# Layer one's pair 2 moved from lone periods into the teams, in a kernel of channel attention and two GLU layers

## The chip, the core and the metric

One NeuronCore of a Trainium2 chip runs the whole program. The metric is the device time of one execution in microseconds; the time of before is the median of three runs, 1169.1 us (1168.38 to 1170.15). Engines are named as in the profile: PE is TensorE's matmul, DVE VectorE, ACT ScalarE, POOL GpSimd, SP the engine that issues most DMAs.

## The reference

There are 6016 tokens with 256 channels. Three things follow each other:

```python
qn = q / (norm(q, axis=1) + 1e-6); kn = k / (norm(k, axis=1) + 1e-6)
a = softmax(kn.T @ qn / tau); x = v @ a              # 256 x 256 attention over channels
x = rmsnorm(x) * rms_g                               # layer one: d_ff = 1536
x = (silu(x @ w_gate) * (x @ w_val)) @ w_out
x = (sigmoid(x @ w2_gate) * (x @ w2_val)) @ w2_out   # layer two: d_ff = 1536
```

All is float32. PE multiplies in a split form: each operand is a high part (float32r) and a low rest, and a product is three matmuls (high x high, high x low, low x high; `mm3`).

## The kernel before, in words

**Blocks, pairs, tiles of weights.** The 47 tiles of 128 tokens form twelve blocks of 512 (block 5 has 384). Two blocks are a pair; pair 2 has 448 columns in each half (`hw`), the others 512. The hidden width is cut into NF = 12 tiles f of 128.

**Stages.** First the attention (until about 104 us), then layer one's pairs 0 and 1 as *plain items*: 48 items (block, f), each with 12 matmuls for gate and value and, two items later (SKEW), 6 for the output. The items of blocks 0 and 1 alternate, then come blocks 2 and 3. Under the plain items the weights of both layers are converted (`conversion`: from 64-bit numbers to float32 by ACT and DVE, sums of weight blocks by POOL, then high by ACT and low by DVE). The steps of a conversion stand in five groups (`ORDER`); a deque `steps` holds the groups of all conversions, and `quota` (lines 1171 to 1181) says how many groups an item pumps, from what is left until item `end`, and from when each tile of layer one is due. Hooks hang further work on single items.

**Double blocks.** Every other pair of both layers is computed with Winograd's form of Strassen's product: seven products (A11, S1, S2, A12, S3, S4, A22) in place of eight. A period is one (layer, pair, f). Seven products of three matmuls are 21 matmuls. The intermediate values live in PSUM banks Z, B, A, D; between two products that use one bank, ACT copies it out (`cpA`, `cpG`, `cpD` and so on).

**Lone and team periods.** Layer one's pair 2 (`PLAIN = 2`) runs first, in twelve lone periods (`period`, line 772). The hidden values are split into parts, and the output layer is computed directly, 4 x 3 = 12 matmuls per f. These periods also prepare layer one's six output weight pairs and the first three of layer two: `out_load`, `out_high`, `out_low`, `out_sums`, with stores to `od`; and they store layer one's weights (`store_w`). Then come nine pairs in *teams* (`team_period`, line 843): six f are one team, and its output product too has Winograd's form, 7 kinds x 3 products x 3 = 63 matmuls per six f. A team's output products run during the six periods after it. So the first six team periods have none of their own; they follow the list `NONE`, and the odd ones take their Z and B from the spare `at` banks. The weights of a team period are read from DRAM two periods ahead (`gw_load`, into three tiles), those of the output product by `ow_load`; partial sums of hidden values go by accumulating DMAs from POOL (`more`, line 604).

**What sets the order.** Everything is emitted in a hand-written order; each engine works its queue in that order, and SP issues DMAs in that order too, so an issue that waits holds all behind it. `slots` hang the next pair's loads, sums and splits and the output weights on points of a period (`early`, `ACT`, `DVE`, `end`).

## Time and profile before

| what | us |
|---|---|
| median of three runs | 1169.1 |
| the profiled execution | 1170.04 |
| its span, first to last instruction | 1168.3 |
| PE busy | 1148.7 |
| DVE busy | 968.3 |
| ACT busy | 890.2 |
| POOL busy | 334.3 |

A busy PE is not a PE at its peak: matmuls are pipelined and counted with their overlap, so the distance between their starts tells more. An idle time stands in brackets with the instruction that ended it. TensorE's granted clock was 0.996 over the span.

### The profile page before, as it was taken

How to read it: one execution, taken by the hardware profiler on the slowest of the kernel's cores; microseconds unless marked ns; L12 is line 12 of the kernel's file. 1: busy time of each engine (PE TensorE's matmuls, PEld its weight loads, DVE VectorE, ACT ScalarE, POOL GpSimd, SP SyncE). 2: the span in 40 equal slices, each digit the busy share in tenths (PEclk: the TensorE clock that was granted, in tenths of full speed). 3: DMA queues.
4: the chain of work that ended last, by engine and by line, in shares of the span. 5: the costliest groups of instructions: out<-in, count | busy, mean ns of one | idle time of the engine just before them, and what ended most of it. 6: DMA issues, size and time to landing. Idle time of an engine off the chain costs nothing.

```text
span 1168.3 us, 16678 instructions
## 1 busy us (share of the span) xinstructions
PE 1148.7 (98%) x5236; PEld 957.0 (82%) x5236; DVE 968.3 (83%) x1496; ACT 890.2 (76%) x1664; POOL 334.3 (29%) x398
## 2 busy tenths in 40 slices
PE   8899999999999999999999999999999999999998
PEld 7788788888898778888888788888888888888896
DVE  6798999886667688888888887888888888888877
ACT  6666788775577687887787887787787787787685
POOL 0043677454223322321321321311311321321121
PEclk9899999999999999999999999999999999999999
DMA  9663445867489989999999998998998998998995
GB/s 329 241 220 143 145 148 190 282 228 238 145 280 322 355 258 266 303 264 266 303 262 272 300 258 251 287 265 245 288 265 240 293 260 247 293 261 245 284 273 147
DMA packets 142856, 296.84 MB, mean 254 GB/s; under 512 B 13872, under 2 KB 53168, under 8 KB 142768
## 3 DMA queue, kind: packets, MB, share of 16 engines
q1 hardware_dynamic: 122032, 258.65, 65.6%
q0 software_dynamic: 20592, 37.00, 18.1%
q8 instruction: 41, 0.67, 0.2%
q14 instruction: 47, 0.39, 0.1%
q10 hardware_dynamic: 144, 0.13, 0.0%
HBM read 201.98 MB, written 56.75 MB: 221 GB/s over the span
## 4 chain that ended last, share of the span: by engine, by line
PE 84%; DVE 8%; DMA 4%; issue 2%; ACT 2%; POOL 1%; SPq 0%; DVEq 0%; POOLq 0%; ACTq 0%
PE g L107 12%; PE g L109 12%; PE g L108 12%; PE v L107 6%; PE v L108 6%; PE v L109 6%; PE y L108 5%; PE y L109 5%; PE y L107 5%; PE at L108 4%; PE at L107 4%; PE at L109 4%; DMA in<-in_q_dram 1%; PE y L973 1%; DVE xn L329 1%
## 5 line engine op out<-in xcount | busy, mean ns | idle before, releaser
L605 POOL DMA_DIRECT2D hs<-hs x143 | 124.7, 918 | 571.5 <-DVE hl L688 413.6
L688 DVE TENSOR_TENSOR hl<-hs,hh 128x512 fp32r<-128x512 f32 (+1 forms) x319 | 221.1, 704 | 25.1 <-ACT hh L657 24.2
L657 ACT CAST hh<-hs 128x512 fp32r<-128x512 f32 (+1 forms) x319 | 192.6, 615 | 25.7 <-PE at L109 6.5
L874 ACT COPY v<-g 128x512 f32<-128x512 f32 (+1 forms) x210 | 119.0, 567 | 63.1 <-PE g L109 59.8
L879 DVE TENSOR_TENSOR hs<-g,e 128x512 f32<-128x512 f32 (+1 forms) x105 | 71.5, 681 | 66.5 <-ACT v L874 65.6
L107 PE MATMUL g<-xh,gw 128*128 128x512 f32 x240 | 94.1, 392 | 0.7 <-DVE hs L879 0.6
L108 PE MATMUL g<-xl,gw 128*128 128x512 f32 x240 | 93.5, 389 | 0.0
L109 PE MATMUL g<-xh,gw 128*128 128x512 f32 x240 | 93.4, 389 | 0.0
L908 ACT ACTIVATE g<-g 128x512 f32<-128x512 f32 (+1 forms) x108 | 67.5, 625 | 30.4 <-DVE g L912 29.4
L107 PE MATMUL y<-hh,ow 128*128 128x512 f32 (+1 forms) x211 | 81.7, 387 | 0.2 <-issue 0.2
L108 PE MATMUL y<-hl,ow 128*128 128x512 f32 (+1 forms) x211 | 81.7, 387 | 0.0
L109 PE MATMUL y<-hh,ow 128*128 128x512 f32 (+1 forms) x211 | 81.6, 387 | 0.0
L874 ACT COPY g<-g 128x512 f32<-128x512 f32 (+1 forms) x105 | 61.3, 583 | 26.2 <-PE g L109 25.8
L912 DVE TENSOR_TENSOR g<-g,g 128x512 f32<-128x512 f32 (+1 forms) x105 | 70.3, 669 | 5.7 <-PE g L109 5.7
L883 ACT ACTIVATE sg<-v 128x512 f32<-128x512 f32 (+1 forms) x108 | 64.2, 594 | 7.5
L107 PE MATMUL g<-qh,gw 128*128 128x512 f32 (+1 forms) x171 | 66.5, 389 | 0.7 <-DVE hs L879 0.6
L109 PE MATMUL g<-qh,gw 128*128 128x512 f32 (+1 forms) x171 | 65.8, 385 | 0.0
L108 PE MATMUL g<-ql,gw 128*128 128x512 f32 (+1 forms) x171 | 65.8, 385 | 0.0
L108 PE MATMUL at<-hl,ow 128*128 128x512 f32 (+1 forms) x160 | 62.4, 390 | 0.6 <-DVE hl L688 0.6
L107 PE MATMUL at<-hh,ow 128*128 128x512 f32 (+1 forms) x160 | 62.2, 389 | 0.3 <-ACT hh L657 0.2
L109 PE MATMUL at<-hh,ow 128*128 128x512 f32 (+1 forms) x160 | 61.9, 387 | 0.0
L874 ACT COPY e<-g 128x512 f32<-128x512 f32 (+1 forms) x105 | 61.3, 584 | 0.4
(256 smaller groups left out, 3312.4 us busy)
## 6 DMA issues: line engine op xcount, KB each, us to landing
gw<-gd SPq DMA_DIRECT2D x216, 448.0 KB, 5.6
ow<-od SPq DMA_DIRECT2D x126, 384.0 KB, 5.4
hs<-hs POOLq DMA_DIRECT2D x128, 256.0 KB, 7.7
wraw<-in_w_dram SPq DMA_DIRECT2D x24, 768.0 KB, 5.3
od<-o SPq DMA_DIRECT2D x48, 256.0 KB, 4.6
vraw<-in_v_t_dram SPq DMA_DIRECT2D x11, 512.0 KB, 4.9
gd<-w2h SPq DMA_DIRECT2D x12, 448.0 KB, 2.6
gd<-w2l SPq DMA_DIRECT2D x12, 448.0 KB, 3.6
```

Source lines behind the costliest of these rows:

```text
L107: nc.tensor.matmul(ps, sh, mh, start=start, stop=False, skip_group_check=more)
L108: nc.tensor.matmul(ps, sh, ml, start=False, stop=False, skip_group_check=more)
L109: nc.tensor.matmul(ps, sl, mh, start=False, stop=stop, skip_group_check=more)
L329: nc.vector.tensor_scalar_mul(xn[b][:, i], ps[i // 2][:, i % 2], rs[:, i : i + 1])
L605: nc.gpsimd.dma_start(out=to, in_=t, accum_op=ALU.add)
L657: nc.scalar.copy(h, src)
L688: nc.vector.tensor_sub(lo, src, f32(h))
L874: nc.scalar.copy(new(name, make, *args), s[src])
L879: nc.vector.tensor_add(s["v1"], s["Z"], s["e5"])
L883: nc.scalar.activation(out=new("sg0", lambda: t), in_=s["A"], func=acts[l])
L908: "gate": lambda: nc.scalar.activation(out=pv["g1"], in_=pv["g1"], func=acts[pl]),
L912: "g1": lambda: nc.vector.tensor_add(s["g1"], s["g1"], s["B"]),
```

## The change

The lone periods and all that served them (`period`, `parts`, `store_w`, `lent_in`) are deleted. Layer one's pairs run in teams in the order 3, 4, 5, 2; layer two is as before. Pair 3's first period follows the plain items directly and has no predecessor; it also runs the last two output products of the plain items. Layer one's weights are stored for the teams during the plain items: the four sums as they are made (`stored`), the rest by hooks. The conversion makes S3 in its own tile, copies all four sums in one instruction, moves `signed` one group ahead, and loads weights three conversions ahead. Of layer one's output weights the direct halves are stored from where they lie (`store_out`), the sums are made under hooks of items 22 to 40. The first three output weight pairs of layer two hang on periods 0, 2 and 4. `end` moves from item 43 to item 42.

```diff
-    NQ = 9
-    S1, S2, S4, A11, A12, A21, A22, OUT = range(8)
+    LATE = 0
+    NQ = 10
+    S3, S1, S2, S4, A12, A11, A22, A21, OUT = range(9)
+    NS = A12
+    NG = A21
+    NW = NQ - NS
...
     ORDER = (
-        "-high units shifted", "-low", "whole signed", "size -s_high -s_low rounded", "guarded sums -stored"
+        "-high units shifted",
+        "-low signed",
+        "whole",
+        "size -s_high -s_low rounded load",
+        "guarded sums -stored",
     )
...
+            for e, t in enumerate((w["sh"], w["sl"])):
+                if l:
+                    nc.sync.dma_start(out=gd[l][f][:, e], in_=f32(t))
+                else:
+                    nc.sync.dma_start(out=gd[l][f][:, e, :NS], in_=f32(t[:, :NS]))
...
-    alone = [(0, PLAIN, f) for f in range(NF)]
-    joint = [(0, p, f) for p in range(PLAIN + 1, NP) for f in range(NF)]
+    SOON_AT = (0, 2, 4)
+    joint = [(0, p, f) for p in (*range(PLAIN + 1, NP), PLAIN) for f in range(NF)]
     joint += [(1, p, f) for p in (0, 1, 3, 4, 5, 2) for f in range(NF)]
-    stream = alone + joint
...
     NONE = (
-        "11 S1 cpA gate h1 P4 third part1 T2 e5 12 flush h0 first"
-        " gw early part0 out out cpG ACT out sg T3 cpD out S4 end"
-        " DVE g1 v1"
+        "11 S1 cpA gate h1 P4 third T2 e5 12 flush h0 first gw early out out cpG ACT out sg T3 cpD out S4 DVE g1 v1 end"
     ).split()
...
         def out():
-            if outs:
-                outs.popleft()()
-                outs.popleft()()
+            if plain:
+                plain.popleft()()
             else:
                 out_product()
...
+            "gw": lambda: n and gw_load(n + 2),
...
         for step in (EVEN, ODD)[n % 2] if n >= HALF else NONE:
-            do.get(step, partial(at, step))()
+            if pv or step not in ("gate", "h1", "P4", "h0", "first"):
+                do.get(step, partial(at, step))()
...
-        end = len(items) - 5
+        now = len(items) - LATE
+        end = now - 6
...
+        def store_plain(f):
+            for e, t in enumerate((wh[0, f], wl[0, f])):
+                nc.sync.dma_start(out=gd[0][f][:, e, NS:], in_=f32(t[:, : NG - NS]))
+        def store_out(f):
+            g, j = divmod(f // 2, NJ)
+            for e, t in enumerate((wh[0, f], wl[0, f])):
+                nc.sync.dma_start(out=od[0][g][:, f % 2 * 2 : f % 2 * 2 + 2, e, j], in_=f32(t[:, 2 * KC :]))
         for f in range(NF):
-            hook(at[2 * PLAIN - 1, f], load_s3, f)
+            hook(at[1, f] + 1, store_plain, f)
+            hook(at[2 * PLAIN - 1, f], store_out, f)
+        for u, n in enumerate([22, 25, 28, 31, 34, 37]):
+            hook(n, out_load, 0, u)
+            hook(n + 2, out_sums, 0, u)
+            hook(n + 3, out_high, 0, u, 4)
+            hook(n + 3, out_low, 0, u, 4)
+        for n in range(3):
+            hook(at[2 * PLAIN - 1, n] + 4, gw_load, n)
...
+        def soon_halves(n):
+            if n < len(soon_pairs):
+                for first in (0, 4):
+                    out_high(*soon_pairs[n], first)
+                    out_low(*soon_pairs[n], first)
+            if n + 2 < len(soon_pairs):
+                out_load(*soon_pairs[n + 2])
+            if n + 1 < len(soon_pairs):
+                out_sums(*soon_pairs[n + 1])
...
+        def plain_out(n):
+            b, f = items[n]
+            for c in range(KC):
+                out_mm(0, b // 2, b % 2, f, c)
+            if f == NF - 1:
+                for c in range(KC):
+                    evacuate(0, b // 2, b % 2, c, c, f32(hidden("hh")))
...
+            if n in SOON_AT:
+                slots[0].setdefault("end", []).append(partial(soon_halves, SOON_AT.index(n)))
...
-            if n in (NF + 1, NF + 2):
+            if n in (3, 4):
                 ow_load()
                 ow_load()
```

## Rows read from the trace of the kernel before

**Rows 1.** The page's busy time, share of the span and instructions.

```profile
PE 1148.7 (98%) x5236; PEld 957.0 (82%) x5236; DVE 968.3 (83%) x1496; ACT 890.2 (76%) x1664; POOL 334.3 (29%) x398
```

**Rows 2.** PE in order of time, first lone period: start us, us, instruction.

```profile
304.23 0.36 PE L107 MATMUL g<-xh,wh 128*128 128x448 f32 x1
304.43 0.37 PE L108 MATMUL g<-xl,wh 128*128 128x448 f32 x1
...
305.24 0.36 PE L109 MATMUL g<-xh,wl 128*128 128x448 f32 x1
305.61 0.47 PE L107 MATMUL g<-xh,wh 128*128 128x448 f32 x1
305.92 0.36 PE L108 MATMUL g<-xl,wh 128*128 128x448 f32 x1
```

**Rows 3.** The table by stretch, two plain ones and the lone stage.

```profile
core 0: us, PE busy (x) PEld busy (x) DVE busy (x) ACT busy (x) POOL busy (x), PEclk, DMA share, GB/s
170.00:204.00 34.00, 34.00 (x152) 28.15 (x151) 33.34 (x44) 27.90 (x49) 23.00 (x30) 1.00 0.53 184
204.00:238.00 34.00, 34.00 (x150) 27.81 (x149) 29.89 (x40) 25.40 (x44) 18.21 (x27) 1.00 0.83 278
304.23:387.09 82.86, 81.61 (x394) 73.10 (x393) 57.63 (x94) 61.06 (x121) 27.03 (x40) 1.00 0.86 290
```

**Rows 4.** PE in order of time, last lone output products; idle time in brackets.

```profile
390.54 0.37 PE L107 MATMUL at<-hh,wh 128*128 128x448 f32 x1
391.10 0.47 PE L108 MATMUL at<-hl,wh 128*128 128x448 f32 x1 [0.19 <-DVE hl L769]
...
392.21 0.45 PE L107 MATMUL y<-hh,wh 128*128 128x448 f32 x1
392.86 0.47 PE L108 MATMUL y<-hl,wh 128*128 128x448 f32 x1 [0.19 <-DVE hl L769]
```

**Rows 5.** ACT in order of time, first team period.

```profile
392.05 0.59 ACT L874 COPY g<-g 128x512 f32<-128x512 f32 x1
392.52 0.55 ACT L507 COPY yo<-at 128x448 f32<-128x448 f32 x1
```

**Rows 6.** ACT in order of time, around the end of a short team period.

```profile
406.48 0.57 ACT L874 COPY v<-at 128x512 f32<-128x512 f32 x1 [0.87 <-PE at L109]
...
408.47 0.59 ACT L874 COPY g<-at 128x512 f32<-128x512 f32 x1 [0.40 <-PE at L109]
```

**Rows 7.** DVE in order of time, last attention block.

```profile
109.03 1.66 DVE L329 TENSOR_SCALAR xn<-at,rs 128x256 f32<-128x256 f32 x4 [1.19 <-POOL rs L323]
110.60 0.95 DVE L158 SCALAR_TENSOR_TENSOR wbits<-wraw,wbits 128x768 uint32<-128x768 uint32 x1
```

**Rows 8.** PE in order of time, weight tile 2.

```profile
120.30 0.50 PE L109 MATMUL g<-qh,wl 128*128 128x512 f32 x1 [1.11 <-DVE wl L195]
```

**Rows 9.** DVE in order of time, low parts of items 16 and 22.

```profile
181.19 0.68 DVE L480 TENSOR_TENSOR hl<-v,hh 128x512 fp32r<-128x512 f32 x1
...
203.17 0.68 DVE L480 TENSOR_TENSOR hl<-v,hh 128x512 fp32r<-128x512 f32 x1
```

**Rows 10.** PE in order of time, v banks of items 16 and 22 used again.

```profile
182.55 0.39 PE L107 MATMUL v<-qh,wh 128*128 128x512 f32 x1
...
207.05 0.40 PE L107 MATMUL v<-qh,wh 128*128 128x512 f32 x1
```

**Rows 11.** DVE groups by form, 212 to 303 us: busy, mean ns, idle before, releaser.

```profile
L478 DVE TENSOR_TENSOR v<-v,sg 128x512 f32<-128x512 f32 x22 | 15.4, 698 | 13.9 <-PE v L109 12.6 <-ACT sg L477 0.7
...
L166 DVE SCALAR_TENSOR_TENSOR wst<-wst,wbits 128x768 f32<-128x768 f32 x8 | 12.0, 1494 | 0.0
```

**Rows 12.** Line 166, DVE's guarded step: ns min/median/max, first and last start.

```profile
L166 DVE SCALAR_TENSOR_TENSOR wst<-wst,wbits x24: 947/1176/1673, 55.1 to 275.2; 128x768 f32<-128x768 f32 x24
```

**Rows 13.** Line 571, the first of POOL's four sums: ns min/median/max.

```profile
L571 POOL TENSOR_TENSOR o<-o x12: 457/624/909, 311.5 to 630.9; 128x128 f32<-128x128 f32 x12
```

**Rows 14.** DMA of 387 to 420 us, the short team periods.

```profile
DMA packets 6585, 11.17 MB, mean 339 GB/s; under 512 B 509, under 2 KB 3713, under 8 KB 6582
```

More of the change, by code (lines that the diff above doesn't have):

```diff
@@ L100 @@
     od = [[dram.tile([P, 8, 2, NJ, P], F32, name=f"od{l}{g}") for g in range(2)] for l in range(2)]
-    s3d = [dram.tile([P, 2, P], F32, name=f"s3d{f}") for f in range(NF)]
     def f32(ap):
@@ new lines, in sums_high @@
+            nc.scalar.copy(h[:, :NS], w["t"][:, :NS])
+        def sums_low():
+            if not l:
+                w["sl"] = cv2.tile([P, NG, P], F32R, tag="w2l", name="w2l")
+            h, lo = w["sh"], w["sl"]
+            nc.gpsimd.tensor_sub(lo[:, :NS], w["t"][:, :NS], f32(h[:, :NS]))
+        def stored():
+            for e, t in enumerate((w["sh"], w["sl"])):
[3 more added lines that the diff above has]
+                    nc.sync.dma_start(out=gd[l][f][:, e, :NS], in_=f32(t[:, :NS]))
@@ L245, in queue @@
             now = named(*conversion(*tile_of)) if tile_of else {}
+            if i + 3 < len(conversions):
+                now["load"] = partial(load_w, *conversions[i + 3])
             for group in ORDER:
@@ L852, in team_period @@
         slot = slots.popleft() if slots else {}
-        outs = deque(partial(out_mm, *o, c) for o in outs for c in range(KC))
         if n and n % HALF == 0:
@@ L1181, in quota, with halves @@
             return most
-        first = stream[0][:2]
-        for n, it in enumerate(items):
+        def halves(l, i, first):
+            steps = [partial(out_high, l, i, first), partial(out_low, l, i, first)]
+            return steps if first else [*steps, partial(out_sums, l, i)]
+        def soon_halves(n):
[7 more added lines that the diff above has]
+                out_sums(*soon_pairs[n + 1])
+        first = joint[0][:2]
+        for n, it in enumerate(items[:now]):
             if n == end:
@@ L1205, with plain_rest @@
                 fn()
-            if n > end:
-                for i in in_turn[2 * (n - end) - 2 : 2 * (n - end)]:
+            ready = n - end - 2
+            if ready >= 0:
+                for i in in_turn[2 * ready : 2 * ready + 2]:
                     pair_high(*first, i)
                     pair_low(*first, i)
-        def halves(l, i, first):
-            steps = [partial(out_high, l, i, first), partial(out_low, l, i, first)]
-            return steps if first else [*steps, partial(out_sums, l, i)]
-        def out_weights(l, i, one, two):
-            for slot, first in ((one, 0), (two, 4)):
-                slot.setdefault("end", []).extend(halves(l, i, first))
-        def store_w(f):
-            for e, t in enumerate((wh[0, f], wl[0, f])):
-                nc.sync.dma_start(out=gd[0][f][:, e], in_=f32(t[:, :NG]))
-        early = {3: [(0, 2)], 4: [(0, 3)], 5: [(1, 0)], 6: [(1, 1)], 7: [(0, 4)], 8: [(0, 5), (1, 2)]}
-        out_load(0, 0)
+        def plain_out(n):
[5 more added lines that the diff above has]
+                    evacuate(0, b // 2, b % 2, c, c, f32(hidden("hh")))
+        def plain_rest(n):
+            plain_one(items[n], 1, True)
+            plain_h(items[n])
+            for fn in hooks.get(n, ()):
+                fn()
+        for n in range(now, len(items)):
+            plain.extend((partial(plain_one, items[n], 0), partial(plain_rest, n), partial(plain_out, n - SKEW)))
+        plain.extend(partial(plain_out, n - SKEW) for n in range(len(items), len(items) + SKEW))
         pv = None
-        outs = [(0, b // 2, b % 2, f) for b, f in items[-SKEW:]]
-        for n, it in enumerate([*stream, None]):
+        for n, it in enumerate([*joint, None]):
             if it and it[2] == 0:
@@ L1230 @@
                 slots.extend({} for _ in range(NF))
-                if n <= len(alone):
-                    done = outs[-1][:2]
-                    for e in range(2) if pv else (1,):
-                        point = slots[0].setdefault("ACT", []) if e and pv else slots[1].setdefault("early", [])
-                        point.extend(partial(evacuate, *done, e, c, c) for c in range(KC))
-                if n + NF < len(stream):
-                    nxt = stream[n + NF][:2]
+                if n + NF < len(joint):
+                    nxt = joint[n + NF][:2]
                     own = ((n // NF) % 2) == 1
```

235 lines of the change are left out of this document (71 added, 164 removed), and 8 rows, old and new, of tables (EVEN, ODD).

## The prediction

> **What bounds the kernel now.** I read the busy shares first: PE is busy for 1148.7 us of a span of 1168.3 [rows 1]. The reader should not trust the 98% by itself, since pipelined matmuls overlap in that count; so the next view is the order of time on PE, where the distance from one start to the next is the price of a matmul. Inside a run without waits of 448 columns it is 0.20 us [rows 2]. The table by stretch then says where more than that is spent [rows 3]. In the plain stage (items 0 to 47) 150 to 152 matmuls per 34 us come to 0.227 us each: no waits, though DVE is busy for 33.3 of 34 us in the first of the two stretches shown. In the twelve lone periods of pair 2, the third stretch, the count is short of the time. So PE bounds nearly everywhere, and time comes only from fewer matmuls or from the few waits of PE. The profiled execution took 1170.0 us (span 1168.3); the median of the runs is 1169.1, 0.9 lower. I make the sum against the profiled one and take 0.9 off.
>
> **Matmuls that go.** A lone period issues 7 products x 3 = 21 matmuls and 2 halves x 2 columns x 3 = 12 output matmuls, 33 in all. In teams six periods share 7 kinds x 3 products x 3 = 63 output matmuls, 10.5 each, so 31.5. Twelve periods of pair 2 change from 33 to 31.5: 18 matmuls of 448 columns, at 0.202 (0.20 by the starts) **-3.6 us**. This part has no other value.
>
> **Waits that go with the lone stage.** The third stretch of the table, 82.9 us, goes from the first lone matmul to just before the first team matmul [rows 3]. It holds 12 x 33 - 3 = 393 matmuls (the first period has no fourth product; the row counts one more that reaches into it), of which 12 have 512 columns: 12 x 0.227 + 381 x 0.202 = 79.7 us. The 3.2 us over are PE waiting for the hidden parts (ACT high, DVE low) and for an evacuation that the lone stage put on its path; that code is deleted. The first team period still carries the last lone output products: there the starts are 0.56 and 0.65 us apart where 0.20 is the pitch, which is 0.8 over, and 0.1 to refill after each as at 305.61; together 1.0 [rows 2, 4]. **-4.2 us**, if nothing takes their place.
>
> **What the new first period costs.** It has no predecessor, so no fourth product lies between the first product and the third, which waits for ACT's copy of Z: I take 0.3 us, the first lone period's own such wait (the starts at 305.24, 305.61 and 305.92 are 0.37 and 0.31 us apart, 0.27 more than two pitches [rows 2]). Then the last two plain output products run in it, and the second brings the evacuation of two banks, one on ACT, queued ahead of ACT's copy of Z to g1. The next product overwrites Z and must wait for both: before, the evacuation stood behind that copy, and the two took 0.55 and 0.59 us [rows 5]. Evacuation, copy, two wake-ups of about 0.1 and the refill 0.1, less the 0.2 that a matmul needs anyway: **+1.3**, between 1.0 and 2.2; behind the evacuation only ACT's sigma and its copies queue. With the 0.3 it is +1.6.
>
> **The three weight pairs of layer two** (end of periods 0, 2, 4: two ACT copies of 0.57, two DVE subtractions of 0.68, four POOL operations, four stores, a load). In such a short period ACT idles 0.87 us before its copy of Z and 0.40 before the copy to g1 [rows 6]. 1.15 us more of ACT (two of the 0.57 there) overfills the first gap by 0.3, and the second gap swallows it; PE's next use is behind three products. DVE has similar holes. I take +0.3 for three periods, between 0 and 1.5.
>
> **The conversion.** Moving "signed" one group ahead puts it into the pump of the last attention block. DVE there idles 1.19 us for POOL before the scaling at 109.03; "signed" (0.95) then runs at 110.60 on the path [rows 7], at whose end PE waits 1.11 us for the low part of weight tile 2 [rows 8]. In the gap it costs nothing: **-0.8**, between 0 and -1.0.
> The groups of five steps, their DVE content and the deadline differ little, but worked through with the planner's formula, three steps per item last until item 20 instead of 15, and the last step falls in item 40 instead of 42. The tightest place before is item 16: DVE's low part ends at 181.19 + 0.68 = 181.87, and PE reuses that v bank at 182.55, 0.68 us later [rows 9, 10]. By the sums of the DVE steps, the changed kernel stands 1.0 us better there and up to 2.2 worse at items 19 to 23, where there is room: at item 22 the same reading gives 203.17 + 0.68 and 207.05, a lead of 3.2. So PE stays unhindered.
>
> **The output weights of layer one.** Six ACT copies and six subtractions vanish with the lone stage (the direct halves are stored from where they lie); six of each and 24 POOL operations move to items 24 to 40. Per 34 us that is 2.7 subtractions of 0.68 for DVE [rows 9], whose 29.9 us of 34 [rows 3] become 31.8, a little less with the narrower low parts of layer two: it fits. DVE spends 13.9 us between 212 and 303 waiting ahead of the product with the gate, nearly all of it for PE [rows 11]. The unknown is the contact with POOL: the guarded step takes 0.95 us at best and 1.18 in the median, 1.67 at most [rows 12], and the slow ones lie on POOL operations. The 24 moved ones take 0.46 to 0.91 [rows 13]. At best nothing is lost (0), at worst each holds DVE for 0.55 (its mean of 1.49 in the late plain stage, less 0.95 [rows 11, 12]): 13 us, plus six waits of 0.6 for the ACT half and 4 of own work, against some 8 us of idle (4.1 of each 34) and the small lead of item 16, so up to 12 us. I take **+0.4**, near the lower end, since POOL is idle for nearly half of that time (18.2 us busy of 34 [rows 3]).
> The Trainium skill (SBUF — State Buffer, "SBUF: two separate sides") says that a DVE instruction with two SBUF inputs and a GpSimd one lock each other out for the whole instruction. The spread of [rows 12] agrees in so far as the step stretches; by that rule, with every pair meeting, the time would be the 1175 of the last rival.
>
> **Transfers.** Twelve more periods read weights (0.9 MB each) and team output weights, but the teams' full periods, half as long again as the short ones (31.5 matmuls for 21), have nearly no waits of PE. The tight place is the six short periods: before, 11.17 MB went in 33 us, 339 GB/s [rows 14]. After, I count 11.3 MB there: six weight pairs 5.4, the next pair 1.0, twelve od stores 3.1, a load 0.25, output weights 1.5. SP also has to issue four stores per soon pair ahead of the next weights, and waits for DVE in front of them. What was stored in the lone stage until 387 is now done earlier, in stretches that move 184 to 278 GB/s [rows 3], so the queue starts emptier. **+0.5**, between 0 and 7.
>
> **Sum:** -3.6 - 4.2 + 1.6 + 0.3 - 0.8 + 0.4 + 0.5 = -5.8; 1170.0 - 5.8 - 0.9 = **1163.3 us**, against 1169.1. All lower ends give -7.9 + 1.3 - 1.0 = -7.6, 1161.5.
>
> **Rivals.** *The waits come back in pair 2's teams.* With 448 columns a full period lasts 31.5 x 0.202 = 6.4 us for 31.5 x 0.227 = 7.2, but the next pair's splits keep 512. Against it: DVE's operations shrink with the columns as PE's do. If 1 to 4 of the 4.2 us return: 1164.5 to 1167.5; chance 0.17.
> *The six short periods become bound by transfers.* If their 11.3 MB go at the 278 GB/s of the second plain stretch [rows 3] rather than at 339, they take 40.6 us for 33: +7, less the 0.5 in the sum: 1170. Against it stands that 339 was reached in the same place. Chance 0.09, about half of it within 0.2% of before.
> *Slower: the lock of DVE and POOL in items 24 to 40.* Place: each of 24 POOL sums meets a two-input DVE step and each of six added subtractions waits for its ACT half. Price up to 12 us, which gives 1163.3 - 0.4 + 12 = 1175; it decides from the item where DVE's idle time and its lead on the v bank are used up. For it speaks L166's spread [rows 12], against it DVE's idle time [rows 11]. Chance 0.05.
> *The change does not do what it says:* the deleted lone stage leaves no way for that, only for smaller terms; I give 0.02 to the rest. The forecast has 0.67.
>
> **How the numbers follow.** A measurement here can tell about 0.2%, 2.3 us, from no change: faster is below 1166.8. The forecast and most of the first rival lie there: 0.83. Within 0.2%: what is left of the first rival and half the second and more: 0.12. Slower: the lock, 0.05. The range takes the lower ends (1161.5, with half a us for the estimates) and the first rival: 1161.0 to 1168.0.
>
> **What would show it.** Right: 18 matmuls fewer; one wait of about 1.3 us in front of the fifth product (T3) of the first team period; no other PE wait over 0.5 us between 120 and 340; the wait at 118 for weight tile 2 down to some 0.3. Wrong: PE waits on v banks in items 19 to 40 with stretched DVE steps beside POOL sums; a wait of PE for weights (a transfer ending it) in periods 3 to 7; PE gaps in the teams of pair 2. If the sum holds in the stages but the total does not, I missed a stage outside these.

## The result, and the profile after

The changed kernel takes 1180.8 us (median of four, 1178.43 to 1182.84) where before takes 1168.7 beside it (1167.59 to 1170.15): ratio 1.0102, 95% interval 1.0077 to 1.0127. It is 1.0% slower. The forecast was 1163.3, range 1161.0 to 1168.0. Two of e8's ten executions, 2947 and 4725 us, stand far from the rest and in no comparison; no run shows what held them.

Where the 12 us lie is read by stages. The marks are starts of PE's matmuls: the first plain one, the first one of a double block, and one in the first period of layer two's second pair. The third column so holds layer one's double blocks and the twelve periods of layer two's first pair, in which layer one's last output products run; the text and the expectations call it layer one's double blocks. All in us, from one profiled execution each (the two lines for the mended kernel are two executions of the same code):

| kernel | before the plain items | plain items | layer one's double blocks, to layer two's second pair | rest | span |
|---|---|---|---|---|---|
| before | 104.81 | 199.42 | 421.35 | 442.68 | 1168.26 |
| changed | 100.94 | 211.34 | 421.99 | 442.37 | 1176.64 |
| e1 | 103.42 | 213.01 | 422.92 | 442.25 | 1181.61 |
| e2 | 104.75 | 205.58 | 420.29 | 442.42 | 1173.05 |
| e3 | 100.52 | 206.70 | 421.71 | 442.19 | 1171.12 |
| e4 | 101.36 | 207.10 | 422.13 | 442.61 | 1173.20 |
| e5 | 104.19 | 209.50 | 418.14 | 442.68 | 1174.50 |
| e6 | 101.33 | 209.76 | 423.05 | 442.49 | 1176.62 |
| e7 | 103.13 | 209.60 | 423.31 | 442.44 | 1178.48 |
| e12 (two edits) | 100.59 | 202.50 | 422.35 | 442.41 | 1167.85 |
| e8 (mended) | 103.15 | 200.60 | 418.83 | 442.69 | 1165.28 |
| e11 (mended) | 105.11 | 200.55 | 418.40 | 442.33 | 1166.38 |
| e9 | 105.49 | 200.66 | 420.97 | 442.15 | 1169.27 |
| e10 | 101.41 | 200.64 | 420.47 | 442.45 | 1164.96 |

Two things stand in it. The plain items are 11.9 us longer, where -0.4 was forecast (-0.8 for the conversion, +0.4 for the output weights). The double blocks of layer one, where nearly all of the gain was to come from, are 0.6 longer and not some 5.4 shorter. The first column is no part of the change: it varies from execution to execution of any kernel. And some waits are followed by a stretch of lower clock that costs 1.7 us. It falls into the plain items in e1, e4 and e5, and into the double blocks in e3, e4, e6 (twice) and e7 to e12; the executions of before, of the changed kernel and of e2 have none in these two columns (both matters at the end). The plain items of e6 have the code of the changed kernel and took 209.76 for its 211.34, so what an experiment gains in that column is known to some 1.6 us. Two kernels are told apart here by the waits of PE in a place more than by a stage's total.

The page of the changed kernel, its busy times, against [rows 1]:

```profile
PE 1144.5 (97%) x5218; PEld 950.0 (81%) x5218; DVE 991.1 (84%) x1524; ACT 890.3 (76%) x1654; POOL 339.1 (29%) x390
```

The 18 matmuls are gone, PE is busy for 4.2 us less, and the span is longer: PE waits more. The two plain stretches of [rows 3], in the changed kernel:

```profile
170.00:204.00 34.00, 31.84 (x137) 24.98 (x136) 33.19 (x40) 25.33 (x42) 21.05 (x24) 1.00 0.78 261
204.00:238.00 34.00, 33.80 (x147) 27.11 (x145) 30.42 (x41) 23.20 (x40) 18.52 (x27) 1.00 0.94 327
```

PE gets through 137 matmuls where it did 152. DVE is as full as before (33.2 of 34 us) and does 40 instructions for 44: the same engine, slower steps. The idle ahead of DVE's product with the gate, the slack of [rows 11], fell from 13.9 us to 3.9 in 212 to 303:

```profile
L477 DVE TENSOR_TENSOR v<-v,sg 128x512 f32<-128x512 f32 x21 | 14.5, 689 | 3.9 <-PE v L110 3.9
```

**What DVE loses, in one item.** DVE and POOL in order of time in the changed kernel, with the matmul that waits for it:

```profile
172.98 1.56 POOL L207 TENSOR_TENSOR w2l<-wst,w2h 128x512 fp32r<-128x512 f32 x1 [2.31 <-ACT w2h L201]
173.30 1.66 DVE L149 TENSOR_SCALAR wbits<-wraw 128x768 uint32<-128x768 uint32 x1
174.89 0.68 DVE L477 TENSOR_TENSOR v<-v,sg 128x512 f32<-128x512 f32 x1
175.49 1.03 DVE L195 TENSOR_TENSOR wl<-wst,wh 128x768 fp32r<-128x768 f32 x1
176.44 1.22 DVE L159 SCALAR_TENSOR_TENSOR wbits<-wraw,wbits 128x768 uint32<-128x768 uint32 x1
177.58 0.68 DVE L479 TENSOR_TENSOR hl<-v,hh 128x512 fp32r<-128x512 f32 x1
...
178.31 0.50 PE L108 MATMUL v<-qh,wh 128*128 128x512 f32 x1 [1.44 <-DVE hl L479]
```

And the same item before:

```profile
173.51 1.39 POOL L209 TENSOR_TENSOR wl<-wst,wh 128x384 fp32r<-128x384 f32 x1 [2.20 <-ACT wh L200]
174.03 1.29 DVE L148 TENSOR_SCALAR wbits<-wraw 128x768 uint32<-128x768 uint32 x1
...
175.24 0.69 DVE L478 TENSOR_TENSOR v<-v,sg 128x512 f32<-128x512 f32 x1
175.84 1.04 DVE L195 TENSOR_TENSOR wl<-wst,wh 128x768 fp32r<-128x768 f32 x1
176.80 0.68 DVE L480 TENSOR_TENSOR hl<-v,hh 128x512 fp32r<-128x512 f32 x1
```

Columns are as in [rows 7]. Two parts of the change meet here. First, POOL's low part of the four sums is now one instruction of 1.56 us and not one of 1.39 and a shorter one behind it (a part of the change that its listing leaves out); DVE's shift (the first step of a conversion on DVE, L148 before and L149 now), which starts while it runs, is held until it is through: 1.66 for 1.29. Second, "signed" (L159) now stands in the group of the low part (L195), and an item pumps such a group between its product (L477) and its own low part (L479): the way from the one to the other was 175.24 to 176.80, 1.56 us, and is 174.89 to 177.58, 2.69. PE's next v bank (the PSUM bank of the value product, free again when the low part is made) hangs on it, and PE waits 1.44. Over all 24 conversions, ns min/median/max of the shift, in the kernel before, the changed one and e12 (POOL's work in two parts, and "signed" back in its place), one fence each:

```profile
L148 DVE TENSOR_SCALAR wbits<-wraw x24: 550/637/1381, 43.7 to 269.2; 128x768 uint32<-128x768 uint32 x24
```

```profile
L149 DVE TENSOR_SCALAR wbits<-wraw x24: 552/850/1659, 42.8 to 274.4; 128x768 uint32<-128x768 uint32 x24
```

```profile
L149 DVE TENSOR_SCALAR wbits<-wraw x24: 549/706/1380, 42.4 to 265.5; 128x768 uint32<-128x768 uint32 x24
```

The shift takes 0.55 us at best and ends 0.4 us behind POOL's instruction in both items shown. The Trainium skill (SBUF — State Buffer, "SBUF: two separate sides") says that of a GpSimd instruction and a DVE one that is in a two-port mode, or has two SBUF inputs while GpSimd reads SBUF, whichever starts first has the shared ports for its whole length. These rows agree, 1.66 beside 1.56; the shift has one input, so the rule needs a two-port mode for it, and no row shows an instruction's mode.

**The output weights.** From item 25 on a second cause shows. ACT's half of each moved pair has its fixed place in the queues, and the first one's load landed late. POOL, ACT, DVE and PE of the changed kernel:

```profile
232.43 0.46 POOL L573 TENSOR_TENSOR o<-o 128x128 f32<-128x128 f32 x1 [2.58 <-DMA o<-rd]
...
234.53 0.62 ACT L556 CAST oh<-o 128x512 fp32r<-128x512 f32 x1 [3.39 <-POOL o L576]
...
235.19 0.69 DVE L560 TENSOR_TENSOR ol<-o,oh 128x512 fp32r<-128x512 f32 x1 [3.45 <-ACT oh L556]
...
239.79 0.50 PE L108 MATMUL v<-qh,wh 128*128 128x512 f32 x1 [1.71 <-DVE hl L479]
```

**The seam**, where the double blocks follow the plain items. PE's waits of over 0.5 us from item 47, the last one, to the fifth product (T3) of the first double period, and what they go back to on SP, POOL and ACT:

```profile
287.21 1.00 SPq L528 DMA_DIRECT2D gw<-gd  x2
...
293.32 4.44 SPq L365 DMA_DIRECT2D xl<-xd  x4
...
301.67 1.29 POOL L405 TENSOR_TENSOR xs<-xl 128x512 f32<-128x512 f32 x1 [13.28 <-DMA xl<-xd]
...
302.99 0.62 ACT L373 CAST xh<-xs 128x512 fp32r<-128x512 f32 x1 [5.05 <-POOL xs L405]
...
307.22 0.50 PE L108 MATMUL g<-qh,wh 128*128 128x512 f32 x1 [1.18 <-ACT sg L476]
309.41 0.50 PE L108 MATMUL v<-qh,wh 128*128 128x512 f32 x1 [0.53 <-DVE hl L479]
313.73 0.50 PE L108 MATMUL g<-xh,gw 128*128 128x512 f32 x1 [0.61 <-ACT sg L476]
316.35 0.50 PE L108 MATMUL g<-xh,gw 128*128 128x512 f32 x1 [1.66 <-ACT v L812]
321.96 0.50 PE L108 MATMUL g<-xh,gw 128*128 128x512 f32 x1 [1.22 <-ACT g L812]
```

Pair 3's four operand loads stand behind the weight loads of two periods on SP (the second at 291.96), and issuing the four takes 4.44 us, of which SP waits 2.8, by its own waits from 284 to 305 us:

```profile
SPq L365 <- DMA gd<-w2h: 2.1, 1, 2.1
SPq L365 <- DMA gd<-w2l: 0.7, 1, 0.7
```

These are two stores that were issued right behind the first weight loads. This program's transfers on SP signal eight semaphores in turn, and an issue waits for the eighth transfer before it to land (so it is for all 717 issues in the changed kernel's trace that have one): the third operand load goes out at 296.36, the store having landed at 296.34, the fourth at 297.44 after 297.43. POOL waits 13.28 us for the first operand, ACT 5.05 for POOL, and the gates of the last items, queued on ACT behind pair 3's high halves, come late. (The first two waits are both in item 47, for its gate bank and its value bank; the expectations put them in items 46 and 47.) Over PE's pitch the five waits are 1.34, 0.69, 0.77, 1.82 and 1.38. The forecast had the last at its size, and the fourth, for ACT's copy of Z, at 0.3.

**The short periods and the first full ones**, whose weights come late (periods are counted from 0; 0 to 5 are the short ones, and these waits lie in periods 3, 6 and 7):

```profile
334.76 0.50 PE L110 MATMUL at<-xh,gw 128*128 128x512 f32 x1 [0.31 <-DMA gw<-gd]
351.44 0.50 PE L110 MATMUL g<-xh,gw 128*128 128x512 f32 x1 [0.80 <-DMA gw<-gd]
360.24 0.50 PE L110 MATMUL g<-xh,gw 128*128 128x512 f32 x1 [0.94 <-DMA gw<-gd]
```

Against the pitch of 0.228 us the three cost 0.47, 0.96 and 1.11: 2.5.

### The profile page after: what moved, and what is told of

Read it like the earlier page. It is cut to its first block, busy times and chain, and to the rows that moved or that the text cites. A ratio compares the mean times of both kernels' runs of the same rounds, so it can differ in the third digit from the quotient of the medians.

```text
span 1176.6 us, 16718 instructions
## 1 busy us (share of the span) xinstructions
PE 1144.5 (97%) x5218; PEld 950.0 (81%) x5218; DVE 991.1 (84%) x1524; ACT 890.3 (76%) x1654; POOL 339.1 (29%) x390
## 4 chain that ended last, share of the span: by engine, by line
PE 66%; DMA 4%; DVE 2%; issue 2%; ACT 1%; POOL 1%; DVEq 0%; SPq 0%; POOLq 0%; ACTq 0%
PE g L108 11%; PE g L110 10%; PE g L109 10%; PE v L108 4%; PE v L110 4%; PE v L109 4%; PE y L108 4%; PE y L110 4%; PE y L109 4%; PE at L110 3%; PE at L108 3%; PE at L109 3%; DMA gw<-gd 2%; DMA hs<-hs 1%; DMA gd<-w2h 1%
## 5 line engine op out<-in xcount | busy, mean ns | idle before, releaser
L607 POOL DMA_DIRECT2D hs<-hs x159 | 138.5, 920 | 626.8 <-DVE hl L690 460.9
L690 DVE TENSOR_TENSOR hl<-hs,hh 128x512 fp32r<-128x512 f32 (+1 forms) x355 | 243.3, 696 | 27.9 <-ACT hh L659 26.6
L659 ACT CAST hh<-hs 128x512 fp32r<-128x512 f32 (+1 forms) x355 | 212.6, 610 | 28.0 <-PE at L110 7.1
L812 ACT COPY v<-g 128x512 f32<-128x512 f32 (+1 forms) x234 | 131.5, 562 | 69.2 <-PE g L110 66.1
L108 PE MATMUL g<-xh,gw 128*128 128x512 f32 x285 | 112.5, 395 | 3.6 <-ACT v L812 1.7
L110 PE MATMUL g<-xh,gw 128*128 128x512 f32 x285 | 111.3, 390 | 1.7 <-DMA gw<-gd 1.7
L109 PE MATMUL g<-xl,gw 128*128 128x512 f32 x285 | 111.1, 390 | 0.0
L108 PE MATMUL y<-hh,ow 128*128 128x512 f32 (+1 forms) x235 | 90.6, 385 | 0.2 <-issue 0.2
L109 PE MATMUL y<-hl,ow 128*128 128x512 f32 (+1 forms) x235 | 90.5, 385 | 0.0
L110 PE MATMUL y<-hh,ow 128*128 128x512 f32 (+1 forms) x235 | 90.4, 385 | 0.0
L108 PEld LDWEIGHTS g<-xh,gw 128*128 128x128 f32 x285 | 53.5, 188 | 19.6 <-ACT v L812 3.1
L108 PE MATMUL at<-hh,ow 128*128 128x512 f32 (+1 forms) x178 | 68.8, 387 | 0.2 <-ACT hh L659 0.2
L110 PE MATMUL at<-hh,ow 128*128 128x512 f32 (+1 forms) x178 | 68.5, 385 | 0.0
```

Of the source, the lines that this page charges most:

```text
L108: nc.tensor.matmul(ps, sh, mh, start=start, stop=False, skip_group_check=more)
L109: nc.tensor.matmul(ps, sh, ml, start=False, stop=False, skip_group_check=more)
L110: nc.tensor.matmul(ps, sl, mh, start=False, stop=stop, skip_group_check=more)
L607: nc.gpsimd.dma_start(out=to, in_=t, accum_op=ALU.add)
L659: nc.scalar.copy(h, src)
L690: nc.vector.tensor_sub(lo, src, f32(h))
```

## The experiments

Times of e1 to e4 stand beside one set of runs of the kernel before, those of e5 to e8 and of e9 to e12 beside another each; ratios are to that.

**e1, the output halves stored early.** The layer's direct output halves are stored in items 4 to 25 and not in the last twelve.

```diff
-            hook(at[2 * PLAIN - 1, f], store_out, f)
+            hook(at[1, f] + 2, store_out, f)
```

> Only the stores of layer one's direct output weight halves move from items 36 to 47 to items 5 to 25. Theory T (transfers): in the changed kernel the queue is full from 287 to 312 us, pair 3's operands land 8 us after their issue, POOL's sums, ACT's and DVE's splits come late, and PE waits 1.3 and 0.7 us in items 46 and 47 and 0.8 and 1.8 us in the first period; the weights of the short periods are late by 0.5 to 1.1 us three times. With 3.1 MB out of that window the four first waits shrink to under 1 us together: the stage from the first plain matmul to the first team matmul goes from 211.3 to about 209, the whole to 1176 or below. Theory L (DVE and POOL lock each other out in the plain items, transfers follow along): the waits in items 46 and 47 and in the first period stay, less than 1 us changes.

Measured: 1180.8 us, ratio 1.0094 (1.0075 to 1.0113); plain items 213.0. The waits in the first double period stay at 0.79, 1.82 and 1.38 us over the pitch (0.77, 1.82 and 1.38 in the changed kernel), and of those in item 47 the second stays, at 0.71, while the first falls from 1.34 to 0.37 (in e6, without this edit, it is 0.71). The stores' bytes at the end of the plain items are not what makes pair 3's operands late.

**e2, no sums of layer one's output weights.** This kernel leaves out the load, POOL sums, ACT copies and DVE subtractions of the six pairs; its stores put the direct halves in their place.

```diff
-            hook(n, out_load, 0, u)
-            hook(n + 2, out_sums, 0, u)
-            hook(n + 3, out_high, 0, u, 4)
-            hook(n + 3, out_low, 0, u, 4)
+            hook(at[2 * PLAIN - 1, u], store_out, u, 4)
```

> Leaves out, in layer one, the sums of the output weights and their split: six loads, 24 POOL sums, six ACT copies and six DVE subtractions under items 22 to 40; the stores of those halves take the direct halves in their place. Theory T: PE's v bank waits at items 32 to 39 (1.9, 0.8, 0.7 us; behind a load that lands late, POOL, ACT and DVE one after the other) vanish, the four v bank waits before item 26 (1.0, 1.6, 0.9, 0.4 us) stay: the plain stage loses 3 to 4 us, to some 207.5. Theory L in its strong form (the added POOL sums are the cause of the plain stage's loss) has 6 us or more vanish, also before item 26. If the late load is not the cause but DVE's own load, only half of the 3.4 us goes.

Measured: 1173.8 us, ratio 1.0037 (1.0024 to 1.0050). The plain items are 5.8 us shorter than in the changed kernel, and still 6.2 longer than before. The waits up to item 26 stay (1.02, 1.61, 0.90 and 0.40 us; 1.00, 1.60, 0.88 and 0.36 in the changed kernel), all those between item 26 and the seam go, and so do the two of item 47; in the double period 0.77, 1.83 and 1.38 stay. So the output weights are about half of the loss, and something ahead of them is the other.

**e3, POOL's low sums in two instructions**, three blocks and one, as before the change.

```diff
-            nc.gpsimd.tensor_sub(lo[:, :NS], w["t"][:, :NS], f32(h[:, :NS]))
+            for s in (slice(0, NS - 1), slice(NS - 1, NS)):
+                nc.gpsimd.tensor_sub(lo[:, s], w["t"][:, s], f32(h[:, s]))
```

> POOL's low part of the four weight sums in two instructions, of three blocks and of one, as it was before the change. Theory L: the one instruction of 1.3 to 1.8 us locks DVE out for its whole length, so that the shift step takes 1.0 us in place of 0.74; with two instructions the shift step falls to 0.75 to 0.85 in the mean and three of the four v bank waits before item 26 (3.8 us together) go: plain stage 208 to 209. Theory O (the order of steps or the quota is the cause, not the length of the lock): shift step and waits stay within 0.5 us.

Measured: 1174.4 us, ratio 1.0036 (1.0024 to 1.0049); plain items 206.7, 4.6 shorter than in the changed kernel. In 110 to 212 us the shift's mean falls from 1145 to 885 ns (810 before) and the guarded step's from 1230 to 1112, although POOL has more to do. So the length of POOL's instruction counts, but the theory's waits don't go: before item 26 three of the four stay, at 0.57, 1.34 and 0.56 us.

**e4, "signed" back behind "whole".**

```diff
-        "-low signed",
-        "whole",
+        "-low",
+        "whole signed",
```

> The sign step goes back behind the shift's own group (the groups of before, with the load in the fourth). Theory: the step ahead of its group did not save 0.8 us, since in the gap before the last scaling it lengthened POOL's power from 1.01 to 1.58 us, so the wait at weight tile 2 stays 1.1 to 1.5 us either way, and the total changes by less than 1 us. Theory O: the early sign step is what makes DVE late in items 2 to 25 (it meets POOL there); then two or more of the 3.8 us of v bank waits go.

Measured: 1175.9 us, ratio 1.0050 (1.0034 to 1.0066); plain items 207.1, 4.2 shorter, with a stretch of lower clock in them:

```profile
117.00:121.00 4.00, 3.44 (x9) 2.71 (x10) 3.75 (x5) 2.73 (x5) 1.79 (x1) 0.57 0.27 64
```

Without its 0.43 x 4 = 1.7 us they are 5.9 shorter. No v bank is waited for up to item 26, though the shift is held as in the changed kernel (mean 1102 ns): theory O came out, with more than it named. PE's wait at the transposes of the last attention block falls from 1.16 to 0.59 us.

**e5, the first weights of the double blocks behind pair 3's operands.**

```diff
-            hook(at[2 * PLAIN - 1, n] + 4, gw_load, n)
+            hook(at[2 * PLAIN - 1, n] + 7, gw_load, n)
```

> Only the three hooks that load the weights of the first three double periods move, from items 40 to 42 to items 43 to 45, so that pair 3's four operand loads stand ahead of them in SP's queue. Theory (the operands are late because six weight loads of 0.45 MB a half stand ahead of them): POOL's wait for xl before the first of pair 3's sums falls from 13.3 us to under 9, ACT's two waits for xs (5.05 and 2.44) shrink, and PE's waits at the seam shrink with them: the g and v banks of items 46 and 47 (1.34 and 0.69 in the changed kernel) to under 0.3 each, the second and third products of the first double period (0.77 and 1.82) to under 0.5 each; the plain stage about 1.7 us shorter, the double blocks of layer one some 2 us: about 1177 where the changed kernel takes 1180.8. Rival 1 (the operands are late because the plain stage's stores fill the DMA engines, wherever the weight loads stand): the waits stay within 0.5 us and the time within 1. Rival 2 (the weights themselves come late then): a new wait of PE for gw of over 1 us before the first product, time 1180 or more.

Measured: 1173.6 us, ratio 1.0049 (1.0029 to 1.0069). Double blocks 418.1, 3.9 us shorter; plain items 1.8 shorter, with 1.7 of lower clock in them. POOL, SP and PE of e5:

```profile
294.41 2.86 SPq L365 DMA_DIRECT2D xl<-xd  x4
...
299.32 1.30 POOL L405 TENSOR_TENSOR xs<-xl 128x512 f32<-128x512 f32 x1 [7.22 <-DMA xl<-xd]
...
320.78 0.50 PE L108 MATMUL g<-xh,gw 128*128 128x512 f32 x1 [1.22 <-ACT g L812]
```

POOL waits 7.2 us and not 13.3, and of the five waits at the seam only the one for the evacuation is left. The theory holds, with a larger gain than it named; its rivals (the bytes of the stores, weights late in their turn) fall. The waits for the weights of periods 3 to 7 also fell, from 2.5 us to 1.3 (0.47 and 0.80).

**e6, the copy to g1 ahead of the evacuation.**

```diff
-        ... "gw early out out cpG ACT out sg"
+        ... "gw early out cpG out ACT out sg"
```

> Only the order of the first double period: the copy of Z to g1 stands ahead of the last plain output product, and so ahead of the two evacuation copies. Theory (the third product waits because the evacuation copy is ahead of the copy on ACT): its wait of 1.38 us falls to under 0.4 (what the kernels of the first call that had slack there show as the copy's own: 0.37), the layer one double blocks get 1.0 us shorter, about 1179.8 in all; everything else as in the changed kernel. Rival (the copy is late whatever stands ahead of it, since ACT is behind by its queue of pair 3's high halves): the wait stays above 1.0 us.

Measured: 1178.9 us, ratio 1.0088 (1.0067 to 1.0109). The wait of 1.38 us, ahead of the fifth product, is gone: it starts at 320.85, the matmul before it at 320.62, a pitch apart. The theory is right there; the double blocks are not 1.0 shorter but 1.1 longer. The weights of period 3 cost 2.2 us (1.78 and 0.46) where those of periods 3, 6 and 7 cost 2.5. The rest is clock, in e6's two stretches of 20 us behind the seam:

```profile
300.00:320.00 20.00, 16.62 (x64) 12.36 (x63) 9.19 (x13) 8.68 (x16) 10.31 (x12) 0.91 0.45 148
320.00:340.00 20.00, 18.10 (x68) 13.12 (x66) 13.93 (x19) 12.59 (x24) 7.92 (x8) 0.91 0.94 280
```

0.09 x 40 = 3.6 us (3.4 by the unrounded clock), where the changed kernel's same stretches have 1.00. Whether the 1.0 us is really won can't be read from so few executions; the wait is gone, the total says no more than 1179 against 1181.

**e7, the output weights loaded two items earlier.**

```diff
-            hook(n, out_load, 0, u)
+            hook(n - 2, out_load, 0, u)
```

> Only the load of each output weight quartet moves, two items earlier, still two items ahead of... its sums four items later instead of two; sums, copies, subtractions and stores as they were. Theory (after item 26 the v banks are late because the load lands late and DVE's subtraction, in its fixed place in the queue, waits for POOL and ACT): DVE's mean wait ahead of the subtraction (6.1 us in six) falls to under 2 in all six, POOL's 6.5 us wait to under 1, and PE's v bank waits behind item 26 (1.87, 0.77, 0.74) and the ones at the end (1.34, 0.69) shrink by 3 us or more in sum: about 1177. Rival (the extra work itself and its lock with POOL fill DVE, with or without a late load): DVE's wait ahead of the subtraction falls but its steps stretch in turn, and PE's waits behind item 26 stay within 1 us of what they were: 1180.

Measured: 1178.2 us, ratio 1.0081 (1.0059 to 1.0103). The first subtraction waits 0.95 us for ACT's high half (235.62 us in e7's trace) where it waited 3.45, and PE's wait of 1.87 us is gone; but DVE's waits ahead of the subtractions in 225 to 292 only fall from 6.1 to 3.6 us, and the other two v banks (0.83 and 0.74 us) and the seam stay. Theory and rival are each half right. What the late load costs is not one number: PE's wait there is 1.87 in the changed kernel, 0.90 in e6 and 2.32 in e5, whose code is the same up to there. So it is 0.9 to 2.3 us of the 5.8, and the plain items of e7 (209.60) are as long as those of e6 (209.76).

**e8 and e11, all five edits of e3 to e7 together** (the mended kernel).

> All five edits together: the four low sums of a conversion on POOL in two instructions, signed back behind whole, the output weights loaded two items earlier, the first three double weights loaded after pair 3's operands, the copy to g1 ahead of the evacuation. Theory (the plain stage loses its 12 us to DVE being held in three places, and the seam 5 us to transfers and queue order; the saving of 7.8 us in matmuls and lone waits is real): plain stage about 201 us (199.4 before, 211.3 in the changed kernel), layer one's double blocks about 417 (421.4 before, 422.0 changed), and the time 1164 to 1167, below both kernels. Rival (the plain stage has not room for 24 POOL sums and twelve more subtractions and copies, in whatever order): plain stage 204 to 206, time 1170 to 1173.

Measured: 1168.25 us (eight executions, 1164.38 to 1171.38) beside 1167.5, ratio 1.0000 (0.9982 to 1.0019), so the time is above the theory's 1164 to 1167. Plain items 200.6, as it said, and double blocks 418.8, 1.8 longer. The second measurement, e11:

> The mended kernel unchanged, for a tighter comparison with the kernel before and with the two others of this call. By its stages (plain 1.2 us more than before, layer one's double blocks 2.5 less) it is 0.1% faster than before: ratio 0.998 to 1.000.

Measured: 1166.7 us (12 executions, 1164.13 to 1169.94) beside 1168.4, ratio 0.9983 (0.9971 to 0.9995). By the two ratios it beats the changed kernel by 1.2%, and the kernel before by 0.17%; e8, of the same code, does not show this last gain, so it is at the edge of what can be told. Plain items 200.6, within 1.2 us of before, with the six moved output weight pairs in them; double blocks 2.5 to 3.0 shorter than before, for 5.4 forecast. What is left there, in e11, PE's waits and the stretch around them:

```profile
324.39 0.47 PE L108 MATMUL at<-xh,gw 128*128 128x512 f32 x1 [1.24 <-DMA gw<-gd]
...
325.43 0.50 PE L110 MATMUL at<-xh,gw 128*128 128x512 f32 x1 [0.34 <-DMA gw<-gd]
```

```profile
320.00:334.00 14.00, 12.42 (x45) 8.92 (x44) 9.33 (x12) 8.40 (x16) 7.95 (x8) 0.88 1.07 339
```

The weights of period 3 cost 1.41 and 0.50 us over the pitch, and the granted clock of those 14 us is 0.88: another 0.12 x 14 = 1.7.

**e9 and e10, the soon pairs (layer two's first three output weight pairs) elsewhere**, in the mended kernel: periods 5, 7 and 9, or 1, 3 and 5.

```diff
-    SOON_AT = (0, 2, 4)
+    SOON_AT = (5, 7, 9)
```

> The mended kernel (all five edits of e8), and layer two's first three output weight pairs moved from periods 0, 2 and 4 to periods 5, 7 and 9. Theory (the third short period waits 2.1 us for its weights because four stores and a load of the first soon pair stand ahead of them in SP's queue, and the clock granted falls to 0.8 for some 8 us behind that wait): the waits for gw in the short periods fall from 2.1 us to under 0.5, the stretch behind them runs at 1.00, and layer one's double blocks take some 415 to 416 us where the mended kernel took 418.8: time 2 to 3 us below the mended one of the same call. Rival (the short periods are bound by the transfers themselves, share 1.0 and over, so that what leaves them comes back as a wait in the periods behind): the waits for gw move to periods 6 to 10, 418 us and no gain.

Measured: 1169.6 us, ratio 1.0006 (0.9994 to 1.0018), double blocks 421.0. In e9 PE waits for no period's weights, but between periods 10 and 11 for something else (and once in period 6, 0.83 us for a low part):

```profile
378.80 0.62 ACT L557 CAST o<-o 128x512 fp32r<-128x512 f32 x1 [3.76 <-DMA o<-rd]
...
380.79 0.50 PE L108 MATMUL g<-xh,gw 128*128 128x512 f32 x1 [3.50 <-DVE g L851]
```

The rival's "no gain" came out, by another wait than it named, and 3 us above its sum: the load of layer two's next output weights, one period ahead of its use, lands late, and ACT, DVE and PE wait some 3.5 us for it. That the moved stores delay it is argued from their place in the queue.

```diff
-    SOON_AT = (0, 2, 4)
+    SOON_AT = (1, 3, 5)
```

> The mended kernel, with the three soon pairs in periods 1, 3 and 5 instead of 0, 2 and 4: the pair's operand loads and the first soon pair no longer stand in the queue together. Theory of the queue's order: the wait of the third short period falls to under 0.8 us, but period 4's weights now stand behind four stores and a load, with some 0.5 us of wait there: 417 us for layer one's double blocks. Rival of the bytes: 418 to 419, the 2 us of waits only one period later.

Measured: 1168.2 us, ratio 0.9998 (0.9985 to 1.0011), double blocks 420.5. The waits move to period 4 (0.75 and 0.47 us) and period 6 (1.43 and 0.99), all for gw (the period's weights), and 420.5 is above what both theories named. In both kernels the transfers are paid for wherever they stand. Of the three places 0, 2, 4 has the lowest median; against 1, 3, 5 the 1.4 us are within the noise of twelve executions each.

**e12, the two edits of e3 and e4 alone.**

> The changed kernel with the two edits against the lock alone: low sums in two POOL instructions, and signed back behind whole. Each alone took the plain stage from 211.3 us to 206.7 and 207.1. If both cure one and the same loss (the lead of DVE over the v banks up to item 26), together they give little more than one: 205 to 207. If they cure two losses that add up, 202 to 203. The theory is the first for the waits before item 26, where e4 already had none, so what is left is behind item 26 (about 1.3 at item 30, 1.1 at 36, 1.9 at the end, by e4): 205.5, time about 1174.

Measured: 1171.8 us, ratio 1.0025 (1.0010 to 1.0039), plain items 202.5. The theory's 205.5 is missed by 3.0. It is half right all the same: alone the two gave 4.6 and, without e4's lower clock, 5.9 us, and together 8.8, less than their sum. Before item 26 they cure the same waits, 3.8 us in the changed kernel, 2.5 in e3 and none in e4 and e12. Behind it e12 has 0.58 on v banks, where e3 has 1.07 and e4 2.38. PE's waits for v banks over the plain items, of the changed kernel and of e12:

```profile
PE v L108 <- DVE hl L479: 6.1, 7, 1.7
```

```profile
PE v L108 <- DVE hl L480: 0.4, 1, 0.4
```

DVE still waits 5.5 us ahead of the output weights' subtractions here, about as in the changed kernel, and behind weight tile 2 and up to item 46 PE waits once, 0.58 over the pitch; the waits of item 47 are 0.99 and 0.70. So with DVE's lead restored (the time by which its low part is ready before PE wants the bank) the moved output weights cost 0.6 to 2.3 us, as one counts these two, which e2 also lost; without it they cost some 5.8. No run has the two edits without the output weights.

## Why the prediction was wrong

- **Matmuls, -3.6: right.** 5236 became 5218.
- **The lone stage's waits, -4.2 "if nothing takes their place": gone, and replaced.** The condition was the weak point. In the mended kernel 2.5 to 3.0 us remain of the gain in the double blocks.
- **The new first period, +1.6: right in one of its two waits.** The wait for evacuation and copy was priced at 1.3 and is 1.38 (e6 takes it away). The third product's wait for the copy of Z was priced at 0.3 and is 1.82. Missed are one of 0.77 ahead of it, and two in item 47, 1.34 and 0.69 over the pitch: the forecast priced the new weight loads as bytes in the short periods, and didn't go through SP's queue for what they are put ahead of. e5, which changes this order alone, takes all four away. The two of item 47 go in e2 as well, so they need the output weights' work too; those of 0.77 and 1.82 stay in e1 and e2.
- **"signed" in the gap, -0.8: much too large, and hidden by another part of the change.** In the gap it runs beside POOL's power, which the row of before has alone. The changed kernel:

```profile
103.88 0.95 DVE L159 SCALAR_TENSOR_TENSOR wbits<-wraw,wbits 128x768 uint32<-128x768 uint32 x1
104.12 1.58 POOL L318 TENSOR_TENSOR rs<-ms,nhalf 128x4 f32<-128x4 f32 x1 [3.10 <-DVE ms L315]
...
116.86 0.50 PE L110 MATMUL g<-qh,wl 128*128 128x512 f32 x1 [1.35 <-DVE wl L195]
```

  and before:

```profile
107.98 1.01 POOL L323 TENSOR_TENSOR rs<-ms,nhalf 128x4 f32<-128x4 f32 x1 [3.11 <-DVE ms L320]
```

  The power takes 1.58 for 1.01, on the path, and the transposes wait 1.16 for 0.60: DVE's idle time there was POOL's time, and not free. The wait of [rows 8] is 1.35 for 1.11 in the changed kernel, but with the low sums in two instructions it is shorter, in e3 ("signed" early) and e12 ("signed" late):

```profile
115.83 0.50 PE L110 MATMUL g<-qh,wl 128*128 128x512 f32 x1 [0.74 <-DVE wl L195]
```

```profile
116.20 0.50 PE L110 MATMUL g<-qh,wl 128*128 128x512 f32 x1 [1.12 <-DVE wl L195]
```

  Counted from the stage's first matmul, the 61st (without the transposes) starts at 19.26 us before, 19.69 in the changed kernel, 19.10 in e3 and 19.38 in e12. So "signed" in the gap gains 0.3 us there, and the merged low sums take 0.6: the forecast's -0.8 for the conversion became +0.4, by a step that it did not price.
- **"So PE stays unhindered": the step that cost most.** It moved the groups' steps by the durations of the old rows and put "worse by up to 2.2" beside room. It did not price the low sums' merging into one POOL instruction, and it took "signed" as one more step in an item, where it stands between an item's product and its low part, the very stretch that [rows 9, 10] showed to be tight: 1.56 us became 2.69. Undoing them takes 4.6 us (e3), 4.2 (e4, 5.9 without its lower clock) and 8.8 (e12) out of the plain items.
- **The output weights, +0.4: right only with a lead.** The bound of "up to 12" held, the choice near its lower end didn't: 5.8 us (e2), 0.9 to 2.3 of it a load that landed late (e7). With "signed" and the low sums as before it is 0.6 to 2.3 (e12). The steps can't be priced one by one: they draw on one slack, the 13.9 us of [rows 11].
- **Transfers, +0.5 between 0 and 7:** the three waits are 2.5, one in the short periods (0.47) and two right behind them. In 321 to 355 us, from the last products of the first double period on, the changed kernel moved

```profile
DMA packets 9318, 10.69 MB, mean 314 GB/s; under 512 B 513, under 2 KB 6657, under 8 KB 9315
```

  for the 11.3 MB and 339 GB/s of the forecast; the place was nearly right, the size too small, and "the queue starts emptier" wrong: 204 to 238 us now has a DMA share of 0.94 for 0.83 [rows 3], and 285 to 300, just ahead of the seam, one of 1.00 for 0.42.
- **The rival of the lock had the mechanism, and a chance of 0.05.** It was placed in items 24 to 40, on the moved POOL sums and the subtractions that wait for ACT. About half of the loss lies there (e2); the other half was decided earlier, in the conversion of items 2 to 25, where [rows 12] had already shown the stretch of the guarded step. Its 1175 is still 6 us short of the 1180.8.
- **The lower ends** add up to -7.5 and not to -7.6 (-3.6 - 4.2 is -7.8); this moves nothing.

In the mended kernel the double blocks are 2.5 to 3.0 us shorter than before, and some 2 of waits for weights and 1.7 of clock are in them. Without these two they would be some 6.4 shorter, by this sum alone and in no run: at least the 5.4 of the forecast. What stays open is how to place the transfers of the short periods so that they cost nothing; three places were tried and none does. Which part of a stretched DVE step is the held start and which another cause is not separated either: e3 and e12 change the length of POOL's instruction and not the meeting itself.

## What to carry to other kernels

Where two engines hold each other up, as DVE and POOL do here, the idle time of one is not free: an instruction put into a gap of DVE or merged on POOL is priced by what the other engine runs in the same microseconds, not by its shortest row. When steps draw on one lead, look for the place where the lead is smallest and ask what now stands between the two instructions that bound it; and when loads are added, go through the issuing queue for what they are put ahead of.

## What the runs showed that was not expected

- A wait of PE can cost more than its length. Behind the 1.8 us ahead of the third product at the seam, e6 (and e3, e4, e7 and e12 alike) shows the granted clock at 0.50, the 1.2 GHz level, for some 3 us:

```profile
315.00:318.00 3.00, 2.82 (x7) 2.25 (x8) 0.44 (x1) 1.22 (x3) 0.00 (x0) 0.50 0.00 0
318.00:321.00 3.00, 3.00 (x14) 2.47 (x13) 0.63 (x1) 0.00 (x0) 0.00 (x0) 0.94 0.00 0
```

  Seven matmuls in 3 us where 13 or 14 are usual: 0.50 x 3 + 0.06 x 3 = 1.7 us. The same waits in the profiled execution of the changed kernel have no such stretch (1.00 throughout 300 to 340). It was the fastest of its four, 1178.4 at a mean clock of 0.999; the second had 0.994 and took 1182.8. So a wait that the forecast prices at its length may cost 1.7 us more, or not.
- The time ahead of the plain items differs by up to 4.9 us between executions (100.59 in e12, 105.49 in e9), with the code up to there the same. In the stretches 30 to 45 and 45 to 60 us the granted clock is 0.92 and 0.85 before and 1.00 in the changed kernel: 0.08 x 15 + 0.15 x 15 = 3.5 us of clock, most of the 3.9 between the two. A single span misjudges a change by that much; a table by stages doesn't.
